# Routed attention and cosine-routed experts: turns of three units instead of two, and the PSUM banks shared out anew

## The chip, the cores and the metric

The kernel runs on one core of a Trainium2 chip. The metric is the device time of one execution in microseconds (us), 787.95 for the kernel before (median of three; 787.69 to 789.35). The engines are TensorE (PE in the profile, PEld for its weight loads), VectorE (DVE), ScalarE (ACT), GpSimd (POOL) and SyncE (SP, which here only issues DMA). Each has its own queue of instructions and they meet through semaphores. [...]

## What is computed

Attention over 4 images (batch) of 8 heads, 768 positions, 64 dimensions; a query sees only those keys that have the same nearest centroid of 16. Its result, as 3072 rows of 512, goes through a router with 8 experts, where one expert per row is taken.

```
q_assign = argmax(q_n . c_n);  k_assign = argmax(k_n . c_n)          # 16 centroids per head
scores   = where(q_assign == k_assign, q k^T / 8, -1e9)
attn_out = softmax(scores) v
x        = attn_out as rows (B*S, H*D) = (3072, 512)
e        = argmax(x_n . emb_n / tau);  gate = softmax(...)[e]
out      = gate * relu(x w1[e]) w2[e]                                # w1 512x1024, w2 1024x512
```

## The kernel before, in words

**Attention.** Two heads form a *pair*, 16 pairs in all (four per image), and each pair is worked in two halves of the queries. One half of one pair is a *group* of six *units*; a unit is 128 keys against 384 queries, of both heads. There are 192 units and 32 groups. For a unit, `scores` (L423) runs on PE: a bf16 product of one-hot numbers `kH` and `H`, which adds the mask, and an f32 product of `kT` and `qT`, into a two-bank PSUM tile `s_ps` (pool psS, two such tiles). `expo` (L445) takes the exponential on ACT into `prob` in SBUF (pool pp, five buffers). `attend` (L450) multiplies `v` with `prob` on PE and adds up over the six units in `o_ps` (pool psO, two banks), and lets DVE add the `prob` up in `acc`.

**A turn.** The main loop (L1003) goes over the units two at a time. In one turn it issues the scores and exponentials of the *next* two units, then what `between` (L935) and `early` (L914) hang into this turn, then `attend` for these two units. So PE has six turns per pair, 96 in all.

**A group's end.** `total` (L479) multiplies ones with `acc` to sum over partitions, into a bank of psM; DVE turns the sums (`sums`, L510) and inverts them (`inv`), POOL copies them to place (L514). `divide` (L519) turns them back (`den`) and forms `xT` from `o_ps`, the mean part `ev` and `den`. In the last three groups, `den` is copied by ACT and inverted whole by DVE (L503). `rows` (L540) turns `xT` and writes it to the DRAM tensor `x_rows`.

**Preparation of the next pair.** `prep_pieces` (L290): `turn0`, `turn1` turn q and k on DVE; `products` (L315) multiplies them with the centroids on PE into a bank of psM, which DVE empties with the transpose `asn` (L328); `choose` (L330) finds the cluster on DVE and writes its number into `cd` on ACT, and a transposing DMA makes `H` (`hot`) of it; `keys` (L372) copies `kH` out of it on POOL; `values` adds v up on POOL.

**Routing.** While image b is attended, image b-1 is routed by `route_pieces` (L554): products with the expert vectors (L559), logits, norms, choose, gates. `Places` (L652) works out where each row stands among its expert's rows; part a covers the first two images and is done in the third and fourth, part b the rest. All PE results of these go into one of the two banks of psM, handed out by `misc()` (L133).

**Experts.** After the last pair, blocks of 128 rows go through `hidden` (w1, L861) and `result` (w2, L880), with `turn_x` (L853) ahead; some 28 blocks are run. `result` sums in a bank of psO.

**What sets the order.** The stretch up to the first expert blocks is written out by hand for all engines (`manual_schedule`, L1001): every engine runs its instructions in the order of the code. The blocks from L1091 on are ordered by a scheduler. PSUM before: psO 2 banks, psM 2, psS 4. When attention is over, psS is given up and its four banks serve the expert part (psX 1, psH 3).

Of the kernel before, what the change touches and what calls it, by code (L numbers as in the profile page):

```python
# [18 lines left out]
P = 128  # L19
# [20 lines left out]
def kernel(  # L40
# [55 lines left out]
    io_i = const.tile([P, P], I32, name="io_i")  # L96
# [22 lines left out]
    xp = ctx.enter_context(tc.tile_pool(name="xp", bufs=2))  # L119
    rta = ctx.enter_context(tc.tile_pool(name="rta", bufs=1))  # L120
    xip = ctx.enter_context(tc.tile_pool(name="xip", bufs=3))
    psO = ctx.enter_context(tc.tile_pool(name="psO", bufs=2, space=PSUM))
    psM = ctx.enter_context(tc.tile_pool(name="psM", bufs=2, space=PSUM))
    at = ctx.enter_context(ExitStack())
    ldp = at.enter_context(tc.tile_pool(name="ldp", bufs=2, side="right"))
    trp = at.enter_context(tc.tile_pool(name="trp", bufs=2, side="right"))
    pp = at.enter_context(tc.tile_pool(name="pp", bufs=5, side="right"))
    ats = ctx.enter_context(ExitStack())
    psS = ats.enter_context(tc.tile_pool(name="psS", bufs=2, space=PSUM, side="right"))

    def misc():  # L133
        return psM.tile([P, 512], F32, tag="misc", name="misc")

    pairs = [(b, hp) for b in range(B) for hp in range(NHP)]
    ld = {}
# [53 lines left out]
    def constants():  # L191
        nc.vector.memset(onesb, 1.0)
        keep_up(9)
        nc.vector.memset(epsc, EPS)
        make_identity(nc, ident)
        nc.gpsimd.iota(io_i, pattern=[[1, P]], base=0, channel_multiplier=0)
# [24 lines left out]
        nc.vector.tensor_scalar(prefc, io_b[:, 0:C], -1.0, float(C), ALU.mult, ALU.add)  # L221
        nc.vector.tensor_scalar(prefe, io_b[:, 0:E], -1.0, float(E), ALU.mult, ALU.add)
# [34 lines left out]
    def begin():  # L257
# [11 lines left out]
        norm_rows(cn_r, c_sb, P)  # L269
        unit_centroids()  # L270
        keep_up(2)
        piece(0, "turn0")
        piece(0, "turn1")
        norm_rows(en_r, emb, E)

        nc.scalar.activation(cn_r, epsc, ACTF.Exp)
        piece(0, "products")
        for m in range(2):
            scores(m, (1,))
        piece(0, "choose")  # L280
        keep_up(6)
        piece(0, "turn_numbers")
        for m in range(2):
            scores(m, (0,))
            expo(m)
        piece(0, "values")
# [126 lines left out]
        }  # L413


    GU = NJ
    units = [(n, hq, j) for n in range(len(pairs)) for hq in range(2) for j in range(NJ)]
    ngroups = len(units) // GU
# [4 lines left out]
    def scores(i, parts=(0, 1)):  # L423
# [1 line left out]
        n, hq, j = units[i]  # L425
        t = ld[n]
        if "s_ps" not in un[i]:
            un[i]["s_ps"] = psS.tile([P, 2, 512], F32, tag="s_ps", name="s_ps")
        s_ps = un[i]["s_ps"]
        for part in parts:  # L430
            if part == 0:
# [18 lines left out]
    def attend(i):  # L450
# [13 lines left out]
        if j == 1:  # L464
            g["acc"] = xp.tile([P, 2, HS], F32, tag="acc", name="acc")
            nc.vector.scalar_tensor_tensor(  # L466
                out=g["acc"],
                in0=un[i - 1]["prob"],
                scalar=NJ * EPS,
                in1=d["prob"],  # L470
                op0=ALU.add,
                op1=ALU.add,
            )
            un[i - 1].clear()
        elif j > 1:
            nc.vector.tensor_tensor(g["acc"], g["acc"], d["prob"], ALU.add)  # L476
            d.clear()

    def total(g):  # L479

# [38 lines left out]
    def divide(g):  # L519
# [8 lines left out]
        if (b, hq) not in xT:  # L528
            xT[b, hq] = xp.tile([P, NHP, HS], F32, tag="xT", name="xT", bufs=3)
        nc.vector.scalar_tensor_tensor(  # L530
            out=xT[b, hq][:, hp],
            in0=d["o_ps"][:, 0:HS],
            scalar=ld[n]["ev"],
            in1=d["den"],
            op0=ALU.add,
# [344 lines left out]
    def result(j, halves=(0, 1)):  # L880
        d = mo[j]
        for half in halves:
            if half == 0:
                d["y_ps"] = psO.tile([P, DM], F32, tag="o_ps", name="y_ps")
            bk = d["y_ps"]
            for c in range(KF // 2 * half, KF // 2 * half + KF // 2):
                nc.tensor.matmul(  # L887
# [24 lines left out]
    prepare, route = {}, {}  # L912
    pa = Places(0, rta)
    early = {  # L914
        (2, 2, 1): pa.ranks,
        (2, 2, 3): pa.firsts,
        (2, 2, 5): pa.experts,
        (2, 3, 1): lambda: pa.dest(0),
        (2, 3, 3): lambda: pa.dest(1),
        (2, 3, 5): pa.hot_blocks,  # L920
        (3, 0, 1): lambda: pa.hot_rows(0, 4),
        (3, 0, 3): lambda: pa.hot_rows(1, 4),
        (3, 0, 5): lambda: pa.hot_rows(2, 4),
        (3, 1, 1): lambda: pa.hot_rows(3, 4),
        (3, 2, 2): pa.tokens,
        (3, 2, 3): lambda: (fetch(0), fetch(1), fetch(2)),
    }

    def piece(n, name, *args):
# [5 lines left out]
    def between(n, it):  # L935
        b, nb = divmod(n, NHP)
        if n == 0:

            if it == 0:
                piece(1, "turn0")  # L940
                piece(1, "turn1")
            elif it == 1:
                piece(1, "products")
                bk = misc()
                piece(0, "mean", bk)
                piece(0, "mean_out", bk)
            elif it == 2:
                piece(1, "choose")
                turned_experts()
        elif it == 0:  # L950
            piece(n + 1, "products")
        elif it == 1:
            piece(n + 1, "choose")
            rows(2 * n - 2)
        elif it == 3:
            rows(2 * n - 1)
        if it == 3:
            piece(n + 1, "keys")
        if it == 4:
            piece(n + 2, "turn0")  # L960
            piece(n + 1, "values")
        elif it == 5:
            piece(n + 2, "turn1")
        if b > 0:
            if nb == 0 and it == 3:
# [3 lines left out]
            m = NJ * nb + it  # L969
            if m in (5, 9, 12):  # L970
                read((m - 5) // 3 * 2, (m - 5) // 3 * 2 + 2)
            if m in (8, 9, 11, 12, 14, 15):
                norms((8, 9, 11, 12, 14, 15).index(m))
            if (nb, it) == (0, 3):
                products(0)
            elif (nb, it) == (0, 4):
                products(1)
            elif (nb, it) == (1, 2):
                logits(0)
            elif (nb, it) == (1, 3):  # L980
                logits(1)
            elif (nb, it) == (1, 4):
                choose()
            if 16 <= m < 20:
                gates[m - 16]()
        if n == NP - 1 and it == 4:
            route[b] = route_pieces(b)
            route[b][2](0, NJ, 0, DM - P)
        if b == B - 1 and (nb, it) == (3, 0):
            for j in range(2):  # L990
                weights1(j)
                weights2(j)
# [7 lines left out]
    }  # L1000
    with tc.manual_schedule(engines=by_hand):  # L1001
        begin()
        for i in range(0, len(units), 2):  # L1003
            n, it = divmod(i // 2, NJ)
# [4 lines left out]
            if it == 3 and n in (1, 2, 3, 5, 6, 7, 9, 10):  # L1009
# [14 lines left out]
            if (b, nb, it) in early:  # L1024
                early[b, nb, it]()
# [7 lines left out]
            if i + 2 == len(units):  # L1033
# [12 lines left out]
        total(ngroups - 1)  # L1046
        divide(ngroups - 1)
        rows(ngroups - 1)
# [114 lines left out]
```

The softmax here doesn't subtract the row's maximum and nothing guards it: scores larger than these inputs give would overflow.

## Time and profile before

The time before is 787.95 us; the profiled execution spans 786.4 us, at a granted clock of 0.997.

| stretch (us) | what runs | PE busy | DVE busy | ACT busy |
|---|---|---|---|---|
| 0 to 20 | constants, first pair's preparation | 14.75 of 20 | 10.52 | 10.11 |
| 100 to 120 | attention, image 1 | 20.00 of 20 | 16.89 | 9.95 |
| 240 to 260 | attention, image 2, places begin | 18.87 of 20 | 19.16 | 13.04 |
| 340 to 360 | end of attention | 19.02 of 20 | 15.30 | 11.56 |
| 460 to 480 | experts | 20.00 of 20 | 1.38 | 2.57 |

The profile tells the busy time of each engine; matmuls are pipelined and their ends are modelled, so what counts for PE is the distance from the start of one to the start of the next. A row like `o_ps<-prob,v 128x384 f32 x8` names the tile written, the tiles read, the shape, and how many instructions were merged. An f32 product appears as two matmuls (two passes). "Idle before <- releaser" tells what an engine waited for.

### The profile page before, as it was taken

To read this page: it belongs to the slowest core of one execution; us is meant where nothing else is said; L and a number is where in the kernel's file an instruction comes from. 1 tells how busy PE (TensorE), PEld (TensorE's weight loads), DVE (VectorE), ACT (ScalarE), POOL (GpSimd) and SP (SyncE) were. 2 spreads that over 40 slices of the span, in tenths; PEclk is the share of its full clock that TensorE was granted. 3 is DMA by queue.
4 is the path that set the end of the run, shared out by engine and by line. 5 is a ranking of instruction groups with operands and counts; after the bars stand their busy time and mean duration, and the time that the engine had idled before them with its cause. 6 is when DMAs were issued, how large, how long until landed. Compare 5 with 4: busy or idle time off the path is not lost.

```text
span 786.4 us, 12732 instructions
## 1 busy us (share of the span) xinstructions
PE 768.4 (98%) x4850; PEld 442.3 (56%) x4850; DVE 349.8 (44%) x614; ACT 259.7 (33%) x417; POOL 183.1 (23%) x402
## 2 busy tenths in 40 slices
PE   7999999999999999999999999999999999999995
PEld 3444444443444334436776776776776776776772
DVE  5688889998889998878430000000000000000000
ACT  5445455564457455563151111111110111111110
POOL 3233323434344233440111211211211211211200
PEclk9999999999999999999999999999999999999998
DMA  9466878877869456485797965988656763146400
GB/s 154 74 131 139 145 110 151 156 148 150 128 140 202 74 92 118 105 248 121 267 332 273 372 226 206 320 320 312 212 220 241 259 244 133 51 143 237 149 15 24
DMA packets 241888, 140.42 MB, mean 179 GB/s; under 512 B 202389, under 2 KB 203925, under 8 KB 241824
## 3 DMA queue, kind: packets, MB, share of 16 engines
q1 hardware_dynamic: 233968, 117.27, 58.5%
q0 software_dynamic: 4480, 13.87, 4.9%
q10 hardware_dynamic: 3376, 8.44, 3.1%
q8 instruction: 40, 0.66, 0.4%
q14 instruction: 24, 0.20, 0.1%
HBM read 158.61 MB, written 13.83 MB: 219 GB/s over the span
## 4 chain that ended last, share of the span: by engine, by line
PE 41%; issue 28%; DMA 23%; DVE 5%; POOL 1%; ACT 0%; SPq 0%; POOLq 0%; DVEq 0%; ACTq 0%
PE s_ps L437 17%; DMA out_dram<-y,sidx 17%; PE o_ps L457 14%; PE h_ps L871 3%; DMA out_dram<-y,gidx 2%; DVE acc L476 2%; PE y_ps L887 2%; PE misc L491 2%; PE misc L319 1%; DMA x_rows<-gate 1%; DMA w1s<-in_moe_w_dram 1%; PE misc L566 1%; DMA w2s<-in_moe_w_dram 1%; DMA q<-in_q_dram 1%; DMA k<-in_k_dram 1%
## 5 line engine op out<-in xcount | busy, mean ns | idle before, releaser
L871 PEld LDWEIGHTS h_ps<-xTm,w1s 128*128 128x128 f32 x1792 | 202.6, 192 | 20.8 <-DVE xTm L859 18.0
L871 PE MATMUL h_ps<-xTm,w1s 128*128 128x128 f32 x1792 | 208.0, 277 | 0.0
L887 PE MATMUL y_ps<-w2s,hT 128*128 128x512 f32 x448 | 201.1, 593 | 0.0
L448 ACT ACTIVATE prob<-s_ps 128x768 f32<-128x768 f32 x192 | 153.8, 810 | 143.1 <-PE s_ps L437 122.4
L859 DVE COPY xTm<-x_ps 128x512 f32<-128x512 f32 x24 | 16.6, 691 | 330.9 <-PE x_ps L857 330.9
L437 PE MATMUL s_ps<-qT,kT 64*128 64x384 f32 x768 | 155.1, 483 | 0.0
L457 PE MATMUL o_ps<-prob,v 128*64 128x384 f32 x768 | 145.1, 499 | 0.8 <-DVE xT L530 0.8
L476 DVE TENSOR_TENSOR acc<-acc,prob 128x768 f32<-128x768 f32 x128 | 129.6, 1012 | 6.4
L887 PEld LDWEIGHTS y_ps<-w2s,hT 128*128 128x128 f32 x448 | 81.0, 190 | 81.8 <-issue 81.8
L878 ACT ACTIVATE hT<-h_ps 128x512 f32<-128x512 f32 x56 | 33.4, 597 | 204.0 <-PE h_ps L871 204.0
L457 PEld LDWEIGHTS o_ps<-prob,v 128*64 128x64 f32 x768 | 46.5, 136 | 84.5 <-issue 69.4
L898 POOL DMA_INDIRECT out_dram<-y,sidx x24 | 23.8, 990 | 290.3 <-ACT y L897 284.4
L514 POOL COPY inv<-inv 32x6 f32<-32x6 f32 x232 | 56.2, 242 | 114.2 <-DVE inv L511 103.5
L437 PEld LDWEIGHTS s_ps<-qT,kT 64*128 64x128 f32 x768 | 68.8, 189 | 20.9 <-issue 20.6
L897 ACT ACTIVATE y<-y_ps,xin 128x512 f32<-128x512 f32 x28 | 19.2, 686 | 146.4 <-PE y_ps L887 140.1
L437 PE MATMUL s_ps<-hot,kH 64*128 64x384 bf16 x384 | 63.5, 328 | 2.3 <-ACT prob L448 1.3
L437 PEld LDWEIGHTS <-kH 64*128 64x128 bf16 x384 | 19.4, 93 | 64.0 <-issue 45.2
L375 POOL COPY kH<-hot 128x768 bf16<-128x768 bf16 x15 | 14.2, 947 | 95.5 <-DMA hot<-cd 83.0
L821 POOL DMA_INDIRECT xin<-x_rows,gidx x28 | 29.8, 1063 | 25.9 <-DMA x_rows<-gate 9.1
L466 DVE SCALAR_TENSOR_TENSOR acc<-prob 128x768 f32<-128x768 f32 x32 | 30.3, 947 | 0.0
L857 PEld LDWEIGHTS x_ps<-ident,xin 128*128 128x128 f32 x112 | 13.9, 141 | 13.8 <-issue 13.2
L491 PE MATMUL misc<-acc,ones 128*32 128x192 f32 (+1 forms) x244 | 18.0, 346 | 2.5 <-DVE acc L476 2.4
(192 smaller groups left out, 413.7 us busy)
## 6 DMA issues: line engine op xcount, KB each, us to landing
w1s<-in_moe_w_dram SPq DMA_DIRECT2D x28, 2048.0 KB
w2s<-in_moe_w_dram SPq DMA_DIRECT2D x28, 2048.0 KB
v<-in_v_dram SPq DMA_DIRECT2D x32, 192.0 KB
x_rows<-xb SPq DMA_DIRECT2D x128, 48.0 KB
q<-in_q_dram SPq DMA_DIRECT2D x60, 96.0 KB
k<-in_k_dram SPq DMA_DIRECT2D x60, 96.0 KB
xr<-x_rows SPq DMA_DIRECT2D x9, 512.0 KB
w1s<-in_moe_w_dram ACTq DMA_DIRECT2D x4, 1024.0 KB
```

Of the source, the lines that this page charges most:

```text
L437: nc.tensor.matmul(s_ps[:, h, 0:HS], lhsT=l[rows, P * j : P * j + P], rhs=r[rows], start=part == (1 if len(parts) < 2 else 0), stop=part = ...
L448: nc.scalar.activation(d["prob"], d["s_ps"][:, :, 0:HS], ACTF.Exp, scale=scale)
L457: nc.tensor.matmul(g["o_ps"][D * h : D * h + D, 0:HS], lhsT=ld[n]["v"][:, j, h], rhs=d["prob"][:, h], start=(j == 0), stop=(j == NJ - 1),)
L466: nc.vector.scalar_tensor_tensor(out=g["acc"], in0=un[i - 1]["prob"], scalar=NJ * EPS, in1=d["prob"], op0=ALU.add, op1=ALU.add,)
L476: nc.vector.tensor_tensor(g["acc"], g["acc"], d["prob"], ALU.add)
L491: nc.tensor.matmul(bk[M * i : M * i + M, 0:W], lhsT=ones[:, 0:M], rhs=d["acc"][:, i * W // HS, c : c + W], start=True, stop=True,)
L514: nc.gpsimd.tensor_copy(inv2[M * to : M * to + M, W // SQ * (i % 2) : W // SQ * (i % 2 + 1)], inv[M * i : M * i + M],)
L821: nc.gpsimd.indirect_dma_start(out=xin, out_offset=None, in_=x_rows[0:n], in_offset=bass.IndirectOffsetOnAxis(ap=gidxs[part][:, c : c + 1] ...
L871: nc.tensor.matmul(bk[:, m : m + P], lhsT=w1s[j % 2][:, c, f0 + m : f0 + m + P], rhs=d["xT"][:, P * c : P * c + P], start=(c == 0), stop=( ...
L878: nc.scalar.activation(d["hT"][:, f0 : f0 + 512], bk, ACTF.Relu)
L887: nc.tensor.matmul(bk, lhsT=d["hT"][:, P * c : P * c + P], rhs=w2s[j % 2][:, c], start=(c == 0), stop=(c == KF - 1),)
L898: nc.gpsimd.indirect_dma_start(out=out[:], out_offset=bass.IndirectOffsetOnAxis(ap=to, axis=0), in_=y, in_offset=None, bounds_check=N - 1, ...
```

## The change

Six units that were three turns become two. A turn has three units; a pair has four turns (NT) and PE 64 in all. For that, psS gets three two-bank tiles (6 banks), and psO and psM keep one bank each. So that the one `o_ps` bank is free for the next group, ACT copies the finished result to SBUF (`o_sb`), and `divide` reads it there. `prob` gets eight buffers. During the start, two of the scores' tiles serve as four spare banks for `misc()`. The pieces in `between` and `early` are hung anew on turns: products and choose of the next pair into turn 0, keys and values into turn 2, the transposes of the pair after into turn 3; the places go one to a turn from the twelfth turn of the third image. `total` and `divide` take turns. When attention is over, the expert part gets two banks of its own for results (psY) from the six of psS. The first product with the expert vectors for the last image moves from the last turn to behind the first half of the first hidden layer. The tile `io_i` moves into a pool that has room at the start.

```diff
-    psO = ctx.enter_context(tc.tile_pool(name="psO", bufs=2, space=PSUM))
-    psM = ctx.enter_context(tc.tile_pool(name="psM", bufs=2, space=PSUM))
+    psO = ctx.enter_context(tc.tile_pool(name="psO", bufs=1, space=PSUM))
+    psM = ctx.enter_context(tc.tile_pool(name="psM", bufs=1, space=PSUM))
...
-    pp = at.enter_context(tc.tile_pool(name="pp", bufs=5, side="right"))
+    pp = at.enter_context(tc.tile_pool(name="pp", bufs=8, side="right"))
...
-    psS = ats.enter_context(tc.tile_pool(name="psS", bufs=2, space=PSUM, side="right"))
+    psS = ats.enter_context(tc.tile_pool(name="psS", bufs=3, space=PSUM, side="right"))
+    spare = []
     def misc():
+        if spare:
+            return spare.pop(0)
         return psM.tile([P, 512], F32, tag="misc", name="misc")
...
+        for bk in (scores_bank(), scores_bank()):
+            spare.extend(bk[:, i] for i in range(2))
         piece(0, "turn0")
         piece(0, "turn1")
...
+    T, NT = 3, 2 * NJ // 3
...
+        if j == NJ - 1:
+            g["o_sb"] = xp.tile([P, HS], F32, tag="o_sb", name="o_sb")
+            nc.scalar.copy(g["o_sb"], g["o_ps"][:, 0:HS])
...
         nc.vector.scalar_tensor_tensor(
             out=xT[b, hq][:, hp],
-            in0=d["o_ps"][:, 0:HS],
+            in0=d["o_sb"],
...
-                d["y_ps"] = psO.tile([P, DM], F32, tag="o_ps", name="y_ps")
+                d["y_ps"] = psY.tile([P, DM], F32, tag="y_ps", name="y_ps")
...
-        (2, 2, 1): pa.ranks,
-        (2, 2, 3): pa.firsts,
-        (2, 2, 5): pa.experts,
-        (2, 3, 1): lambda: pa.dest(0),
-        (2, 3, 3): lambda: pa.dest(1),
-        (2, 3, 5): pa.hot_blocks,
-        (3, 0, 1): lambda: pa.hot_rows(0, 4),
...
+        (2, 11): pa.ranks,
+        (2, 13): pa.firsts,
+        (2, 14): pa.experts,
+        (2, 15): lambda: pa.dest(0),
+        (3, 1): lambda: pa.dest(1),
+        (3, 2): pa.hot_blocks,
+        (3, 3): lambda: pa.hot_rows(0, 4),
...
+        (3, 10): lambda: (fetch(0), fetch(1), fetch(2)),
...
         elif it == 0:
             piece(n + 1, "products")
+            piece(n + 1, "choose")
         elif it == 1:
-            piece(n + 1, "choose")
             rows(2 * n - 2)
+        elif it == 2:
+            rows(2 * n - 1)
+        if it == 2:
+            piece(n + 1, "keys")
+            piece(n + 1, "values")
         elif it == 3:
-            rows(2 * n - 1)
-        if it == 3:
-            piece(n + 1, "keys")
-        if it == 4:
             piece(n + 2, "turn0")
-            piece(n + 1, "values")
-        elif it == 5:
             piece(n + 2, "turn1")
...
-            if 16 <= m < 20:
-                gates[m - 16]()
+            if m in (1, 3):
+                products(m // 2)
+            elif m in (5, 7):
+                logits(m // 2 - 2)
+            elif m == 9:
+                choose()
+            elif m >= 12:
+                gates[m - 12]()
...
-            for m in range(i + 2, min(i + 4, len(units))):
+            for m in range(i + T, min(i + 2 * T, len(units))):
                 scores(m)
                 expo(m)
             between(n, it)
-            if i > GU and i % GU == (2 if i // GU + 2 >= ngroups else 4):
-                divide(i // GU - 1)
...
-            for m in range(i, i + 2):
+            for m in range(i, i + T):
                 attend(m)
-            if i + 2 == len(units):
+            if i > 0 and i % GU == 0:
+                total(i // GU - 1)
+            elif i > GU:
+                divide(i // GU - 1)
+            if last:
                 rows(ngroups - 2)
-                route[b][0](0)
-            if i % GU == 0 and i > 0:
-                total(i // GU - 1)
...
+        psY = ctx.enter_context(tc.tile_pool(name="psY", bufs=2, space=PSUM, **tile_waits))
...
         hidden(0, (0,))
+        products(0)
         total(ngroups - 1)
```

More of the change, by code (lines that the diff above doesn't have):

```diff
@@ L95 @@
     epsc = const.tile([P, 1], F32, name="epsc")
-    io_i = const.tile([P, P], I32, name="io_i")
     io_b = const.tile([P, P], BF16, name="io_b")
@@ L126, with scores_bank @@
     trp = at.enter_context(tc.tile_pool(name="trp", bufs=2, side="right"))
-    pp = at.enter_context(tc.tile_pool(name="pp", bufs=5, side="right"))
+    pp = at.enter_context(tc.tile_pool(name="pp", bufs=8, side="right"))
     ats = ctx.enter_context(ExitStack())
-    psS = ats.enter_context(tc.tile_pool(name="psS", bufs=2, space=PSUM, side="right"))
+    psS = ats.enter_context(tc.tile_pool(name="psS", bufs=3, space=PSUM, side="right"))
+    spare = []
     def misc():
+        if spare:
+            return spare.pop(0)
         return psM.tile([P, 512], F32, tag="misc", name="misc")
+    def scores_bank():
+        return psS.tile([P, 2, 512], F32, tag="s_ps", name="s_ps")
     pairs = [(b, hp) for b in range(B) for hp in range(NHP)]
@@ L195, in constants @@
         make_identity(nc, ident)
+        io_i = xp.tile([P, NJ, DM], F32, tag="xr", name="io", bufs=1).bitcast(I32)[:, 0, 0:P]
         nc.gpsimd.iota(io_i, pattern=[[1, P]], base=0, channel_multiplier=0)
@@ L277, in begin @@
         piece(0, "products")
-        for m in range(2):
+        for m in range(T):
             scores(m, (1,))
@@ L281, in begin @@
         keep_up(6)
+        spare.append(psO.tile([P, 512], F32, tag="o_ps", name="numbers_ps"))
         piece(0, "turn_numbers")
-        for m in range(2):
+        for m in range(T):
             scores(m, (0,))
@@ L427, in scores @@
         if "s_ps" not in un[i]:
-            un[i]["s_ps"] = psS.tile([P, 2, 512], F32, tag="s_ps", name="s_ps")
+            un[i]["s_ps"] = scores_bank()
         s_ps = un[i]["s_ps"]
@@ L914 @@
     early = {
-        (2, 2, 1): pa.ranks,
-        (2, 2, 3): pa.firsts,
-        (2, 2, 5): pa.experts,
-        (2, 3, 1): lambda: pa.dest(0),
-        (2, 3, 3): lambda: pa.dest(1),
-        (2, 3, 5): pa.hot_blocks,
-        (3, 0, 1): lambda: pa.hot_rows(0, 4),
[L922 to L926, printed above, removed]
+        (2, 11): pa.ranks,
[5 more added lines that the diff above has]
+        (3, 3): lambda: pa.hot_rows(0, 4),
+        (3, 5): lambda: pa.hot_rows(1, 4),
+        (3, 6): lambda: pa.hot_rows(2, 4),
+        (3, 7): lambda: pa.hot_rows(3, 4),
+        (3, 9): pa.tokens,
+        (3, 10): lambda: (fetch(0), fetch(1), fetch(2)),
     }
@@ L941, in between @@
                 piece(1, "turn1")
-            elif it == 1:
-                piece(1, "products")
                 bk = misc()
@@ L946, in between @@
                 piece(0, "mean_out", bk)
+            elif it == 1:
+                piece(1, "products")
+                piece(1, "choose")
             elif it == 2:
-                piece(1, "choose")
                 turned_experts()
@@ L951, in between @@
             piece(n + 1, "products")
+            piece(n + 1, "choose")
         elif it == 1:
-            piece(n + 1, "choose")
             rows(2 * n - 2)
+        elif it == 2:
[3 more added lines that the diff above has]
+            piece(n + 1, "values")
         elif it == 3:
-            rows(2 * n - 1)
-        if it == 3:
-            piece(n + 1, "keys")
-        if it == 4:
             piece(n + 2, "turn0")
-            piece(n + 1, "values")
-        elif it == 5:
             piece(n + 2, "turn1")
+        m = NT * nb + it
         if b > 0:
-            if nb == 0 and it == 3:
+            if m == 1:
                 route[b - 1] = route_pieces(b - 1)
             products, logits, read, norms, choose, gates = route.get(b - 1, (None,) * 6)
[L969 to L982, printed above, removed]
+            if m in (3, 6, 9):
+                j = (3, 6, 9).index(m) * 2
+                read(j, j + 2)
+            if m in (5, 6, 8, 9, 11, 12):
+                norms((5, 6, 8, 9, 11, 12).index(m))
+            if m in (1, 3):
[3 more added lines that the diff above has]
+            elif m == 9:
                 choose()
-            if 16 <= m < 20:
-                gates[m - 16]()
-        if n == NP - 1 and it == 4:
+            elif m >= 12:
+                gates[m - 12]()
+        if n == NP - 1 and it == 3:
             route[b] = route_pieces(b)
             route[b][2](0, NJ, 0, DM - P)
-        if b == B - 1 and (nb, it) == (3, 0):
+        if b == B - 1 and m == 12:
             for j in range(2):
@@ L1002 @@
         begin()
-        for i in range(0, len(units), 2):
-            n, it = divmod(i // 2, NJ)
+        for i in range(0, len(units), T):
+            n, it = divmod(i // T, NT)
             if it == 0 and n + 2 < NP:
@@ L1008 @@
                 load(n + 1, "v")
-            if it == 3 and n in (1, 2, 3, 5, 6, 7, 9, 10):
+            if it == 2 and n in (1, 2, 3, 5, 6, 7, 9, 10):
                 slot, part = divmod(n - 1 - n // 4, 4)
@@ L1020 @@
             between(n, it)
-            if i > GU and i % GU == (2 if i // GU + 2 >= ngroups else 4):
-                divide(i // GU - 1)
             b, nb = divmod(n, NHP)
-            if (b, nb, it) in early:
-                early[b, nb, it]()
-            if i + 2 == len(units):
+            if (b, NT * nb + it) in early:
+                early[b, NT * nb + it]()
+            last = i + T == len(units)
+            if last:
                 ats.close()
@@ L1030 @@
                 turn_x(0, nc.scalar.copy, xp.tile([P, DM], F32, tag="acc", name="xTm"))
-            for m in range(i, i + 2):
+            for m in range(i, i + T):
                 attend(m)
-            if i + 2 == len(units):
+            if i > 0 and i % GU == 0:
+                total(i // GU - 1)
+            elif i > GU:
+                divide(i // GU - 1)
+            if last:
                 rows(ngroups - 2)
-                route[b][0](0)
-            if i % GU == 0 and i > 0:
-                total(i // GU - 1)
         at.close()
```

## The prediction

> **What bounds the kernel now.** I read the busy shares first, then the 40 slices, then the matmuls in order of time inside the attention, then the waits, and last the stretch in which attention gives way to the experts.
>
> ```profile
> PE 768.4 (98%) x4850; PEld 442.3 (56%) x4850; DVE 349.8 (44%) x614; ACT 259.7 (33%) x417; POOL 183.1 (23%) x402
> ...
> PE   7999999999999999999999999999999999999995
> ...
> DVE  5688889998889998878430000000000000000000
> ```
>
> TensorE is busy from end to end, so only three things can shorten the kernel: fewer or cheaper matmuls, less lost between matmuls, or the few stalls. VectorE (DVE) is next in the attention (slices 1 to 18), near full in slices 12 to 14, and nearly idle afterwards. This is one turn of the attention as TensorE runs it, two units:
>
> ```profile
> 150.75 0.33 PE L437 MATMUL s_ps<-hot,kH 64*128 64x384 bf16 x2
> 150.91 0.81 PE L437 MATMUL s_ps<-qT,kT 64*128 64x384 f32 x4
> 151.65 1.51 PE L457 MATMUL o_ps<-prob,v 128*64 128x384 f32 x8
> 153.09 0.34 PE L437 MATMUL s_ps<-hot,kH 64*128 64x384 bf16 x2
> 153.27 0.81 PE L437 MATMUL s_ps<-qT,kT 64*128 64x384 f32 x4
> ```
>
> The first column is the start. A plain turn is 3.16 us (151.65 to 154.81 for the next L457). The starts of single matmuls say where it goes: inside a block the next pass starts 0.161 us later for the bf16 mask part and 0.322 us for each f32 pass, so the scores of a unit take 0.161 + 2 x 0.322 = 0.806 us and its attend 2 x 0.322 = 0.645 us. Two units make 2.90; the turn takes 0.26 more. That is lost at the two changes of kind: 0.415 instead of 0.322 from the last score pass to the first attend pass, 0.374 at the next attend pass, 0.425 from the last attend pass back to the scores, and 0.174 for 0.161 at the first mask part: 0.093 + 0.052 + 0.103 + 0.012 = 0.26 us.
>
> Where TensorE really stops is found by the same starts: nine of them between 24 and 352 us come later than the same change does elsewhere, at 180.0 (0.64), 253.1 (0.42), 258.1 (0.85), 266.4 (0.35), 267.5 (0.31), 269.3 (0.71), 336.0 (0.13), 344.6 (0.63) and 347.3 (0.51): 4.5 us. Six of the nine lie at or after the first placing steps. The waits of 240 to 285 us name DVE, which has 19.1 of 20 us busy there:
>
> ```profile
> 240.00:260.00 20.00, 18.87 (x134) 7.86 (x132) 19.16 (x40) 13.04 (x21) 6.13 (x15) 1.00 1.05 192
> 260.00:280.00 20.00, 18.95 (x128) 7.49 (x126) 19.12 (x43) 9.62 (x14) 7.82 (x21) 1.00 0.59 90
> ```
>
> The columns are PE, weight loads, DVE, ACT, POOL. PE is short of 20 just where DVE is full. At the change to the experts nothing stalls today:
>
> ```profile
> 362.67 1.51 PE L457 MATMUL o_ps<-prob,v 128*64 128x384 f32 x8
> 364.11 0.85 PE L566 MATMUL misc<-xT,embT 128*32 128x384 f32 x8
> 364.89 3.84 PE L871 MATMUL h_ps<-xTm,w1s 128*128 128x128 f32 x32
> 368.66 0.87 PE L491 MATMUL misc<-acc,ones 128*64 128x384 f32 x4
> ```
>
> [...]
>
> **The change part by part.**
>
> *Turns of three.* 192 units make 64 turns instead of 96. The matmuls are the same; 32 pairs of changes go: 32 x 0.26 = **-8.3 us**, all on the path. In a pair of heads this is 20.99 to 20.47 us. The extra pieces (products, sums) keep their own changes.
>
> *One result bank, with a copy.* Each of 32 groups gains a 128x384 ScalarE copy, 0.48 us by the row of the den copy from PSUM, 15 us in all on an engine a half busy. The copy follows the group's last attend; the next attend comes after three scores, 2.4 us. Cost nothing: the scores hide it. DVE's divide no longer holds the bank, which removes the 0.63 us stall at 344.6.
>
> *Lighter turns, eight probability buffers, later transposes.* An exponential may now run when DVE is one turn of 4.6 us behind, formerly one of 3.2; sums wait for additions a turn earlier, likewise. The nine stalls should go: **-4.5 us**.
>
> *One bank for others.* Now every user of it waits until the one before has been emptied. I step DVE through a pair of four turns with the starts of its rows: asn .5, choose 2.0, acc .95 per unit, sums .6, rows .5, divide 1.1, the two transposes 1.85. With no routing it ends turns 0 to 3 at 8.3, 12.8, 16.3 and 23.0 us from the pair's start, against TensorE's 6.2, 10.8, 15.9 and 20.5; the next products come at 20.5 + 3.2, so asn is not late and the sums (at 5.4 in turn 0) find the bank empty. In the fourth pair of the third image turn 1 gets the gate scale (1.1) and the first blocks (1.6), turn 3 the gate sum (1.0) and the places (.7): DVE ends it near 27.4, so 6.9 us into the next pair, and empties products at 7.5. The sums behind it wait 2.2 us; the routed products of turn 1 then wait some 1.1 for the sums. The durations overlap by up to a tenth each, so I take 2.5 of the 3.3: **+2.5 us** (bounds 0 and 5).
>
> *Root at the start of a pair.* On ScalarE the two table loads and the root (2.8 us) now stand behind the mask numbers of choose; that puts turn 1's exponentials at about 10.2 us and turn 2's scores want them at 11.0. I take .3 for each of two images: **+0.6** (0 to 2).
>
> *The first pair.* Its keys were wanted six turns after the start with choose in turn 2; now choose is in turn 1 and the keys are wanted in turn 3. From the transposing DMA to the key copy took 4.0 us (28.1 to 32.1), the copy .8. With choose done near 28 the keys stand at 33.1, and TensorE is there at 31.8: **+1.2** (0 to 2).
>
> *The start.* Four spare banks for the first transposes remove the wait at 7.81 us (0.32) and its emptying: **-0.5**.
>
> *The last pair and the hand-over.* The last three divisors use a full reciprocal of 2.55 us on DVE. Its last turns hold three of these and 11.6 us of additions behind in-order waits: the reciprocal of the third-last group starts at 6.2 us into the pair (after the root and the den copy), the additions of turn 1 end at 13.0, the second reciprocal runs 16.1 to 18.7, gate sum and additions end at 22.5, and the divide at 23.0. TensorE has finished its attends and half a hidden layer at 21.5 and wants this for products(0): 1.5. Then the sums of the last group wait for the copy of that bank, 0.3 + 0.48: 0.8. Then products(1) waits for the reduce of logits(0) in the same bank: 0.4. **+2.7 us** (1 to 5).
>
> *Banks for experts.* Two before, two after, in other places; the order of matmuls after the hand-over is the same. Nothing, since y is emptied 7 us before its bank is wanted. The tiles that only moved (io) cost nothing, at the start behind the loads.
>
> Sum: 787.95 - 8.3 - 4.5 - 0.5 + 2.5 + 0.6 + 1.2 + 2.7 = **781.7 us**.
>
> **The rivals.** *All new waits outside the hand-over hide:* 787.95 - 13.3 + 2.7 = 777.4. For it: the longer turns forgive more. Against: DVE has only 1.4 us of slack in a pair. *DVE takes over in the third and fourth image:* only the first two gain from turns (4.2 us) and the stalls stay: 787.95 - 4.2 - 0.5 + 1.2 + 2.7 = 787.2. For it: 19.1 of 20 us. Against: work moves out of that stretch into the fourth image. *Slower:* the single bank is late in each of the 11 other pairs of the routed images, at half of my 2.5 us: 781.7 + 13.8 = 795.5. For it: sums stand right behind products. Against: by my steps asn is there 0.9 us early or more in ordinary pairs.
>
> **How the numbers follow.** Forecast 0.6, all hidden 0.2, DVE-bound 0.12, slower 0.08. The range, 777.0 to 787.5, takes in the first three and the bounds of the unknown waits; about two in ten lie outside, since the bounds can add up. Bounds of no change are 786.4 and 789.5: faster 0.82, same 0.09 (most of the DVE case), slower 0.09.
>
> **What would show it.** Right: a plain turn of 4.61 us; a pair of heads of 20.5; no late starts of the old nine; a wait of the mean or sums for asn in the pair after the places; a late start of the routing products behind the first hidden half. Wrong: late starts at every pair's sums, exponentials held behind the mask numbers, or the attend of a new group waiting for the copy of the old one; and a plain turn over 4.7 us would sink the first term.

## The result and the profile after

The changed kernel takes 793.96 us (793.78 to 794.22) beside 788.19 us of the kernel before on the same chip: a ratio of 1.0071 (95% interval 1.0054 to 1.0089). It is slower by 0.7%; the forecast was 781.7 us. The span of the profiled execution grows from 786.4 to 792.4 us, so the two traces have 6.0 us to explain.

The page of the changed kernel, busy shares and two rows of the 40 slices:

```profile
PE 763.9 (96%) x4850; PEld 449.6 (57%) x4850; DVE 353.9 (45%) x614; ACT 271.5 (34%) x449; POOL 201.5 (25%) x402
...
PE   7999999999999989969999999999999999999995
...
PEclk9999999999999999998999999999999999999998
```

TensorE is busy for 4.5 us less than before, although the span is longer: what was to be saved between matmuls has been saved, and more has been lost in stops. The eighteenth slice (337 to 357 us) has a 6 where the kernel before had a 9, and the granted clock (PEclk) falls in the nineteenth. The same in numbers, per 20 us: PE, weight loads, DVE, ACT, POOL, then the clock, the DMA share and GB/s.

```profile
340.00:360.00 20.00, 13.07 (x78) 6.04 (x76) 8.96 (x14) 9.92 (x15) 4.03 (x10) 0.82 0.72 257
360.00:380.00 20.00, 18.75 (x127) 11.71 (x127) 15.59 (x19) 5.93 (x11) 0.00 (x0) 0.93 0.37 86
```

The matmuls of TensorE, in order of time, show one stop that is larger than the whole loss:

```profile
347.95 2.16 PE L470 MATMUL o_ps<-prob,v 128*64 128x384 f32 x12
357.03 0.51 PE L450 MATMUL s_ps<-hot,kH 64*128 64x384 bf16 x2 [6.93 <-ACT prob L461]
357.31 1.51 PE L450 MATMUL s_ps<-qT,kT 64*128 64x384 f32 x4
```

After an attend the scores normally start 2.1 us later; here it is 9.1, so 7.0 us are lost. (Below, the time given for a stop is the start of the last matmul before it, and its size is how much later than elsewhere the next one starts.) Then four f32 score passes take 1.51 us instead of 0.81: single passes start 0.640 us apart instead of 0.322. That is half the clock (granted clock 0.50), it lasts until 362.9 us, and it costs a further 2.9 us.

The stop can be followed back. TensorE waits for ScalarE's exponentials, which empty the banks of the scores. Here are ScalarE's and then VectorE's instructions of the same stretch:

```profile
345.08 0.21 ACT L637 ACTIVATE sq<-sq 128x6 f32<-128x6 f32 x1
354.38 0.48 ACT L518 COPY den<-misc 128x384 f32<-128x384 f32 x1 [9.09 <-DVE ev L412]
354.88 1.28 ACT L461 ACT_TABLE_LOAD   x1
356.17 2.21 ACT L461 ACTIVATE prob<-s_ps 128x768 f32<-128x768 f32 x3
```

```profile
351.11 0.58 DVE L540 STREAM_TRANSPOSE den<-inv 128x384 f32<-128x384 f32 x1 [10.26 <-POOL inv L530]
351.73 0.62 DVE L546 SCALAR_TENSOR_TENSOR xT<-o_sb,ev,den 128x384 f32<-128x384 f32 x1
352.26 0.95 DVE L479 SCALAR_TENSOR_TENSOR acc<-prob 128x768 f32<-128x768 f32 x1
353.32 0.96 DVE L489 TENSOR_TENSOR acc<-acc,prob 128x768 f32<-128x768 f32 x1
354.19 0.15 DVE L412 COPY ev<-misc 128x1 f32<-128x1 f32 x1
```

ScalarE's exponentials stand behind a table load of 1.28 us and, before that, its copy of the divisor, which waits for VectorE's ev copy, which stands behind a transposition (den) that has waited 10.3 us for the copies of the reciprocals on GpSimd. And these are GpSimd's instructions, after and then before:

```profile
329.64 3.75 POOL L634 TENSOR_TENSOR cumx<-cumx,eq 128x8 bf16<-128x8 bf16 x6
333.33 0.82 POOL L386 COPY kH<-hot 128x768 bf16<-128x768 bf16 x1
334.12 1.31 POOL L395 TENSOR_TENSOR vs<-v 128x384 f32<-128x384 f32 x1
...
337.87 1.99 POOL L837 DMA_INDIRECT xin<-x_rows,gidx  x1 [0.17 <-DVE sums L526]
340.17 1.57 POOL L837 DMA_INDIRECT xin<-x_rows,gidx  x1 [0.31 <-issue]
342.04 1.00 POOL L837 DMA_INDIRECT xin<-x_rows,gidx  x1 [0.30 <-issue]
343.04 0.41 POOL L530 COPY inv<-inv 32x6 f32<-32x6 f32 x2
349.78 1.30 POOL L530 COPY inv<-inv 32x6 f32<-32x6 f32 x6 [6.32 <-DMA xin<-x_rows,gidx]
```

```profile
335.83 1.77 POOL L821 DMA_INDIRECT xin<-x_rows,gidx  x1 [0.17 <-issue]
337.91 1.00 POOL L821 DMA_INDIRECT xin<-x_rows,gidx  x1 [0.31 <-issue]
339.21 0.99 POOL L821 DMA_INDIRECT xin<-x_rows,gidx  x1 [0.30 <-issue]
340.21 0.42 POOL L514 COPY inv<-inv 32x6 f32<-32x6 f32 x2
343.06 1.30 POOL L514 COPY inv<-inv 32x6 f32<-32x6 f32 x6 [2.43 <-DMA xin<-x_rows,gidx]
```

In both kernels the third copy of the reciprocals waits until the tokens that the three fetches bring have landed. Nothing in the source makes the copies need the tokens. The first two copies run right behind the fetches; it is the third that carries, in both traces, waits for the three semaphores that the fetches raise. Why the build puts them there stays open. Before, the wait was 2.43 us. In the changed kernel the fetches are issued 2.0 to 2.8 us later, since the running counts (L634, 3.75 us) and the values' sums (L395 to L397) now stand right ahead of them on GpSimd. They landed at 340.5, 342.2 and 342.9 us before, and land at 342.2, 348.2 and 349.6 now. In between four expert weights of 2 MB each are on the move, issued by SyncE from 338.88 us, before the second fetch; before, the first of them was issued at 340.67, after the third.

### The profile page after: what moved, and what is told of

Same layout as the page of the kernel before. It is cut to its first block, busy times and chain, and to the rows that moved or that the text cites. A ratio compares the mean times of both kernels' runs of the same rounds, so it can differ in the third digit from the quotient of the medians.

```text
span 792.4 us, 12802 instructions
## 1 busy us (share of the span) xinstructions
PE 763.9 (96%) x4850; PEld 449.6 (57%) x4850; DVE 353.9 (45%) x614; ACT 271.5 (34%) x449; POOL 201.5 (25%) x402
## 4 chain that ended last, share of the span: by engine, by line
issue 33%; PE 27%; DMA 21%; DVE 12%; SPq 2%; POOL 2%; ACT 1%; POOLq 0%; DVEq 0%; ACTq 0%
DMA out_dram<-y,sidx 16%; PE s_ps L450 11%; PE o_ps L470 8%; DVE acc L489 4%; PE h_ps L887 2%; DMA out_dram<-y,gidx 2%; PE y_ps L903 2%; DVE acc L479 1%; DMA x_rows<-gate 1%; SPq L162 1%; PE misc L507 1%; DMA k<-in_k_dram 1%; DMA xin<-x_rows,gidx 1%; PE misc L330 1%; DVE xT L546 1%
## 5 line engine op out<-in xcount | busy, mean ns | idle before, releaser
L461 ACT ACTIVATE prob<-s_ps 128x768 f32<-128x768 f32 x192 | 151.0, 813 | 57.1 <-PE s_ps L450 53.1
L450 PE MATMUL s_ps<-qT,kT 64*128 64x384 f32 x768 | 157.0, 488 | 0.0
L470 PE MATMUL o_ps<-prob,v 128*64 128x384 f32 x768 | 138.4, 496 | 0.5 <-ACT o_sb L493 0.5
L489 DVE TENSOR_TENSOR acc<-acc,prob 128x768 f32<-128x768 f32 x128 | 127.2, 994 | 9.5 <-ACT junk L617 0.5
L530 POOL COPY inv<-inv 32x6 f32<-32x6 f32 x232 | 62.3, 269 | 165.1 <-DVE inv L527 150.5
L470 PEld LDWEIGHTS o_ps<-prob,v 128*64 128x64 f32 x768 | 49.6, 137 | 79.0 <-issue 67.4
L479 DVE SCALAR_TENSOR_TENSOR acc<-prob 128x768 f32<-128x768 f32 x32 | 34.3, 1073 | 0.0
L493 ACT COPY o_sb<-o_ps 128x384 f32<-128x384 f32 x32 | 15.4, 480 | 32.9 <-PE o_ps L470 32.8
L395 POOL TENSOR_TENSOR vs<-v 128x384 f32<-128x384 f32 x16 | 21.0, 1315 | 9.7 <-DMA v<-in_v_dram 8.9
L540 DVE STREAM_TRANSPOSE den<-inv 128x384 f32<-128x384 f32 x29 | 16.6, 572 | 13.0 <-POOL inv L530 13.0
```

What stands on the lines that cost most here:

```text
L395: nc.gpsimd.tensor_tensor(vs, v[:, 0 : NJ // 2], v[:, NJ // 2 :], ALU.add)
L450: nc.tensor.matmul(s_ps[:, h, 0:HS], lhsT=l[rows, P * j : P * j + P], rhs=r[rows], start=part == (1 if len(parts) < 2 else 0), stop=part = ...
L461: nc.scalar.activation(d["prob"], d["s_ps"][:, :, 0:HS], ACTF.Exp, scale=scale)
L470: nc.tensor.matmul(g["o_ps"][D * h : D * h + D, 0:HS], lhsT=ld[n]["v"][:, j, h], rhs=d["prob"][:, h], start=(j == 0), stop=(j == NJ - 1),)
L479: nc.vector.scalar_tensor_tensor(out=g["acc"], in0=un[i - 1]["prob"], scalar=NJ * EPS, in1=d["prob"], op0=ALU.add, op1=ALU.add,)
L530: nc.gpsimd.tensor_copy(inv2[M * to : M * to + M, W // SQ * (i % 2) : W // SQ * (i % 2 + 1)], inv[M * i : M * i + M],)
```

## The experiments

Below, "the changed kernel" is at a ratio of 1.0071, and every ratio is to the kernel before in the same batch of runs. Its median lay between 788.19 and 789.74 us from batch to batch, so ratios are the better measure across batches.

### The fetches behind the copies (e1) and the weights a turn later (e2)

```diff
-        (3, 10): lambda: (fetch(0), fetch(1), fetch(2)),
+        (3, 11): lambda: (fetch(0), fetch(1), fetch(2)),
```

> The changed kernel with one edit: the three fetches stand one turn later, at turn 11 of the last image instead of turn 10, so that in GpSimd's queue they come after the copies of the inverted sums of that turn and no such copies follow them. Queue theory (the copies wait for the landing of the fetches, and all else queues behind): the stop of 7.0 us at 349.6 and the half clock after it (some 2.9 us) go, 793.96 becomes about 784.1. Rival (VectorE is full and one bank for others is too few; the fetch only shows it): at most 2 us, about 792. Rival (the root and its table loads in front of the last pair's exponentials): the stop stays at 4 us or more, about 790.

Measured 784.84 us, ratio 0.9943 (0.9929 to 0.9958). Three instructions, one turn later, take 1.28% off, about 10 us (9.1 between the two medians, which come from different batches); the stop and the half clock after it were 7.0 + 2.9 = 9.9. GpSimd in e1:

```profile
338.53 3.65 POOL L530 COPY inv<-inv 32x6 f32<-32x6 f32 x8 [0.27 <-DVE inv L527]
342.48 1.25 POOL L837 DMA_INDIRECT xin<-x_rows,gidx  x1 [0.29 <-POOL inv L530]
...
345.50 1.00 POOL L837 DMA_INDIRECT xin<-x_rows,gidx  x1 [0.30 <-issue]
```

The eight copies run ahead of the fetches, nothing in this stretch waits for a landing, and TensorE has no stop between 329 and 362 us. This shows the cause of the loss: the fetches' place ahead of the copies. e2 leaves the fetches where the change put them and moves the weights:

```diff
-        if b == B - 1 and m == 12:
+        if b == B - 1 and m == 13:
```

> The changed kernel with one edit: the first blocks' weights are asked for one turn later (turn 13 instead of 12 of the last image); the fetches stay. Queue theory: the 8 MB of weights no longer stand in front of the second and third fetch, which land in some 3 us instead of 7.6 after the last was issued; the copies go on 4 us sooner, the stop falls from 7.0 to about 3 us, 793.96 becomes about 789.5 (a little less if the clock then stays whole). Rival (VectorE full, one bank): no change, 794. If the fetches land as late as before, the length of the wait is not the weights'.

Measured 792.65 us, ratio 1.0041 (1.0023 to 1.0060): 1.3 us better, less than expected. GpSimd, then TensorE, then a later line of VectorE and TensorE's wait for it:

```profile
345.99 1.30 POOL L530 COPY inv<-inv 32x6 f32<-32x6 f32 x6 [2.30 <-DMA xin<-x_rows,gidx]
```

```profile
353.24 0.37 PE L450 MATMUL s_ps<-hot,kH 64*128 64x384 bf16 x2 [2.88 <-ACT prob L461]
353.40 1.49 PE L450 MATMUL s_ps<-qT,kT 64*128 64x384 f32 x4
...
377.17 1.42 PE L582 MATMUL misc<-xT,embT 128*32 128x384 f32 x8 [2.57 <-DVE lg L598]
378.52 4.88 PE L887 MATMUL h_ps<-xTm,w1s 128*128 128x128 f32 x32
```

```profile
376.39 0.58 DVE L561 STREAM_TRANSPOSE xb<-xT 128x384 f32<-128x384 f32 x1 [2.56 <-DMA x_rows<-xb]
```

The landing wait falls from 6.3 to 2.3 us, and TensorE's stop from 6.9 to 2.9: so 4 of the 7 us came with the weights in flight, and the rest is the place in GpSimd's queue. But 2.9 us of stop are still followed by the half clock (1.49 us for four passes): the three units' scores take 4.2 us and not 2.5, so 1.7 of the 2.9 us stay. And the weights, now issued from 357.8 us, stand just ahead of the writing of the last rows, which SyncE issues from 361.1: VectorE waits 2.6 us for one of these writes to land, TensorE's second routing products 2.6 instead of 0.3, and half clock follows here too (1.42 us for 0.85, and 4.88 for the 3.84 of the next hidden half). So 4.1 and 1.2 us were gained, 2.2 and 1.6 given back later: 1.5, and 1.3 were measured.

### The same hazard in the kernel before (e5)

```diff
-        (3, 2, 3): lambda: (fetch(0), fetch(1), fetch(2)),
+        (3, 2, 4): lambda: (fetch(0), fetch(1), fetch(2)),
```

> This is the kernel before, with one edit: the first three fetches of tokens are issued one turn (two units) later in the last image, behind the copies of the reciprocals and not ahead of them. Theory (the copies on GpSimd carry a wait for the landing of the fetches, and the two late starts of TensorE near 344.6 and 347.3 us of the kernel before, 1.1 us together, are its end): these two late starts go, the 2.4 us wait of GpSimd and the 2.5 us wait of VectorE go with it, and the time falls by about 1.1 us, a ratio of 0.9986. Rival, which is what the prediction took (these late starts come from the result bank that is freed late, as at the other seven places): both stay, ratio 1.000.

Measured 788.40 us over 21 runs against 789.58, ratio 0.9988 (0.9981 to 0.9995). The late starts near 344.6 and 347.3 us are gone from its trace. (That trace has a stop of its own, 2.6 us near 253 us for GpSimd's copy of the keys, and half clock from 15.6 to 22.4 us, both far from the edit; it is of the longest of the 21 executions.) So the hazard was there already, worth 0.12%, and two of the nine stalls that the prediction booked were its end. The wait that named it (GpSimd for the fetches, 2.43 us) stands in the trace of before, and the prediction doesn't use it.

### The root (e3, e9)

e3 is e1 without the root of the first three images' norms; a copy stands in its place:

```diff
-            nc.scalar.activation(t["sq"], t["sq"], ACTF.Sqrt)
+            nc.scalar.activation(t["sq"], t["sq"], ACTF.Copy if b < B - 1 else ACTF.Sqrt)
```

> The kernel with the later fetch, and the square root of the first three images' norms left out (a copy stands in its place, so no tables are loaded in the attention). If the two table loads behind the mask numbers hold the next exponentials, the late starts of scores at 174.9 (0.6) and 260.1 (1.5) go and the kernel gains about 2.1 us on the kernel with the later fetch. Rival (these scores wait for VectorE's additions to free the probability buffers): no gain, within 0.3 us.

Measured 784.00 us, ratio 0.9930 (0.9912 to 0.9949), 0.8 us less than e1. In e1 the scores start 0.7 and 1.5 us late at 175 and 260 us, behind exponentials that stand behind two table loads; both late starts are gone in e3. But the mean's wait in the last pair of the third image grew from 2.0 to 2.7 us, and 0.4 us appeared at 264. The stops were the root's, and more than half of what it frees is lost again: a few turns later to VectorE, and in this trace to a longer half clock (277.9 to 284.7 us, in e1 280.6 to 284.0). e9 moves the four steps of the gates one turn, away from the turn in which ScalarE waits for the choice of hot keys (it is built on e8, below):

```diff
-            elif m >= 12:
-                gates[m - 12]()
+            elif m >= 13:
+                for gate in gates[m - 13 : m - 12 if m < 15 else None]:
+                    gate()
```

> e8, and the four steps of the gates one turn later (turns 13 to 15 and not 12 to 15, the last two in one turn), so that the root with its two table loads no longer lies in the turn in which ScalarE waits 2 us for VectorE's choice of hot keys. Theory (the root costs TensorE 0.7 and 1.5 us at 174 and 260 us because it adds 2.7 us to a turn in which ScalarE has already lost 2): these stops go, and with the same in the fourth image up to 2.2 us less than e8; since e3 gave back most of what the root's removal freed, at the bank of the last pair, and that bank is now free earlier, 1.3 to 2.2 us less. Rival 1 (two table loads of 1.28 us delay three exponentials wherever they lie): stops of the same size at turn 13, no change. Rival 2 (VectorE, not ScalarE, sets the pace there): the stop returns elsewhere, under 0.8 us less.

Measured 783.56 us, ratio 0.9928 (0.9913 to 0.9944), 0.3 us less than e8, within the intervals. The stops at 174 and 260 us are gone, and 1.1 us each appear at 193 and 279, named for VectorE's sums: the second rival.

### The first pair (e4)

e4 is e1 with the next pair's products and choice put into the first turn of the first pair, and the mean of v one turn later:

```diff
             if it == 0:
                 piece(1, "turn0")
                 piece(1, "turn1")
+                piece(1, "products")
+                piece(1, "choose")
+            elif it == 1:
                 bk = misc()
...
-            elif it == 1:
-                piece(1, "products")
-                piece(1, "choose")
```

> The kernel with the later fetch, and in the very first pair the products and the choice for the second pair one turn sooner (turn 0), the mean part of v one turn later (turn 1). If the second pair's keys are late by the time from the choice through the transposing DMA, the late start at 32.4 (1.1 to 1.25 us) goes and the kernel gains about 1.2 us on the kernel with the later fetch. Rival (the products then wait for the transposes of q and k on VectorE, and the loss only moves): within 0.4 us of it.

Measured 783.64 us, ratio 0.9927 (0.9912 to 0.9941), 1.2 us less than e1. The late start at 32.7 us is gone, as its size said.

### The one bank and VectorE (e6, e8, e10, e11)

In e4 the largest stop that is left in the attention is this, TensorE in order of time:

```profile
274.63 2.16 PE L470 MATMUL o_ps<-prob,v 128*64 128x384 f32 x12
278.71 0.35 PE L402 MATMUL misc<-epsc,vs 128*128 128x1 f32 x2 [1.93 <-DVE asn L339]
...
279.71 1.49 PE L450 MATMUL s_ps<-qT,kT 64*128 64x384 f32 x4
```

The mean waits for the bank, since VectorE empties the products (asn, 277.99) 3.3 us after they were done; then the half clock again. e6 is e4 with the places moved:

```diff
-        (2, 13): pa.firsts,
-        (2, 14): pa.experts,
-        (2, 15): lambda: pa.dest(0),
-        (3, 1): lambda: pa.dest(1),
-        (3, 2): pa.hot_blocks,
+        (3, 0): lambda: (pa.firsts(), pa.experts()),
+        (3, 1): lambda: pa.dest(0),
+        (3, 2): lambda: (pa.dest(1), pa.hot_blocks()),
```

> The changed kernel with the fetches a turn later and the first pair's keys early (e4), and beside these the firsts, experts and destinations of the first two images' places moved out of the last pair of the third image into the first three turns of the fourth: some 4 us of VectorE work leave a stretch in which it is busy without a gap. Theory (the mean waits 2.0 us in the single bank at 277 us because VectorE is late, and the half clock of some 1.6 to 2.9 us behind it follows from that stop): both go, 3.6 to 4.5 us less than e4's 783.6, so 779.1 to 780.0. Rival 1 (the single bank alone makes the mean wait, however early VectorE is): the stop stays, no change, 783.6. Rival 2 (VectorE's work only moves and makes TensorE wait in the fourth image's first turns): one stop is traded for another, 782 to 784.

Measured 782.67 us, ratio 0.9918 (0.9904 to 0.9932), the lowest of all, though its interval overlaps that of e4. The mean comes on time (276.12) and the half clock is gone, but the next user of the bank waits:

```profile
276.12 0.38 PE L402 MATMUL misc<-epsc,vs 128*128 128x1 f32 x2
276.43 0.53 PE L507 MATMUL misc<-acc,ones 128*32 128x192 f32 x8
...
281.17 0.85 PE L582 MATMUL misc<-xT,embT 128*32 128x384 f32 x8 [1.67 <-DVE sums L526]
```

This is rival 2 of its expectation: one stop traded for another. e8 spreads the same steps over turns 1 to 3 of the fourth image:

```diff
-        (3, 0): lambda: (pa.firsts(), pa.experts()),
-        (3, 1): lambda: pa.dest(0),
-        (3, 2): lambda: (pa.dest(1), pa.hot_blocks()),
-        (3, 3): lambda: pa.hot_rows(0, 4),
+        (3, 1): lambda: (pa.firsts(), pa.dest(0)),
+        (3, 2): lambda: (pa.dest(1), pa.experts()),
+        (3, 3): lambda: (pa.hot_blocks(), pa.hot_rows(0, 4)),
```

> e6, with the moved places spread over turns of the fourth image that have no choosing of hot keys: firsts and the first destinations at turn 1, the second destinations and the experts at turn 2, the hot blocks with the first hot rows at turn 3. In e6 the mean's wait of 2.0 us in the one bank had gone, but the route's products, next in the same bank, waited 1.7 us for VectorE, which had 4 us of places between choosing and additions. Theory (whichever use of the one bank meets VectorE late waits, so the work must lie where nothing in the bank is near): the 1.7 us stop shrinks to under 0.5, and the 0.5 us at 291 with it, so 780.5 to 781.3 against e6's 782.7. Rival (VectorE is full over the whole stretch from 252 to 300 us, and the stop only moves on to the next turns): 782 to 783.5.

Measured 783.90 us, ratio 0.9933 (0.9918 to 0.9948): no gain. The stop of 1.7 us is gone, and one of 2.0 stands further on, before the routing's second products, at 289.9 us. The time lies a little above what even the rival gave. e10 (on e9) and e11 (on e8) put the places at the end of their turns, so that the bank's readers stand ahead of them in VectorE's queue:

```diff
-            if (b, NT * nb + it) in early:
-                early[b, NT * nb + it]()
             last = i + T == len(units)
...
             elif i > GU:
                 divide(i // GU - 1)
+            if (b, NT * nb + it) in early:
+                early[b, NT * nb + it]()
```

> e9 (root moved, places spread), and beside it each step of the places goes at the end of its turn, behind the turn's sums or division, and not ahead of its additions. VectorE takes its work in order, so in e9 the sums of the total at 287 us left the one bank only at 292, behind the places and the additions, and the route's products waited 2.1 us. Theory (the one bank costs time where its reader stands behind unrelated work in VectorE's queue; with the reader in front, the same amount of work costs nothing): the 2.1 us and 0.5 us stops at 291 and 304 go, about 2.4 us less than e9's 783.6, so 781.2. Rival (VectorE is full there and TensorE waits for it at another point): 782.5 to 783.6.

> e8 with the same edit of e10 and the root left where it was: the same theory expects about 2.4 us less than e8's 783.9, so 781.5, and the root's late starts at 174 and 260 us (0.9 and 0.8 us in e8) still there; the rival 783 to 784.

Measured 784.12 us (ratio 0.9940, 0.9927 to 0.9954) and 783.82 us (0.9930, 0.9917 to 0.9943). The 2.0 us at 290 us became 0.3 in e11, as the theory has it, but the list of waits of e11 shows where they went:

```profile
PE s_ps L450 <- ACT prob L461: 3.1, 3, 1.9
PE misc L402 <- DVE asn L339: 1.6, 1, 1.6
PE misc L330 <- DVE rka L700: 1.4, 1, 1.4
...
PE misc L595 <- DVE sums L526: 1.1, 1, 1.1
```

The columns are the sum, the count and the longest. The products at 251.7 now wait for the ranks in the bank, and the mean for asn two pairs later. Both times show no gain: the rival's outcome, in e10 0.5 us above its range. The reason that it gives is a full VectorE. Here is the busy time of e9, in which the scores hardly wait for exponentials (0.6 us in all), and below it a stretch of the changed kernel:

```profile
240.00:260.00 20.00, 19.90 (x144) 8.81 (x145) 19.00 (x32) 11.63 (x21) 9.26 (x22) 1.00 0.79 165
260.00:280.00 20.00, 19.25 (x140) 8.31 (x136) 18.93 (x31) 12.94 (x21) 7.44 (x18) 1.00 0.55 91
280.00:300.00 20.00, 17.20 (x126) 7.08 (x128) 18.76 (x48) 10.54 (x16) 7.60 (x21) 1.00 0.81 127
```

```profile
300.00:320.00 20.00, 19.98 (x144) 8.96 (x142) 19.17 (x32) 11.20 (x20) 9.33 (x20) 1.00 0.63 104
```

In e9 VectorE is busy for 56.7 us of 60, and TensorE stops. But from 300 to 320 us of the changed kernel it is busy for 19.17 us of 20, and TensorE hardly stops (19.98). So a full VectorE alone is not enough: it takes a use of the bank whose reader comes late in VectorE's order of work. That both are needed is argued from these traces and not tested by itself. In each of the five arrangements of the same work some use of the bank met a late reader; they lie between 782.7 and 784.1 us, and the lowest and the highest have overlapping intervals. What these runs leave open is how much two banks for others would have saved there: with six banks for scores there is no second one, and it wasn't tried.

### The hand-over (e7)

e7 is e6 with the last total moved:

```diff
         hidden(0, (0,))
         products(0)
+        hidden(0, (1,))
         total(ngroups - 1)
         divide(ngroups - 1)
         rows(ngroups - 1)
-        hidden(0, (1,))
```

> e6, and beside it the last group's total moved behind the second half of the first expert block's hidden layer, so that the one bank for others is free of the route's products when the total comes. Theory (the hand-over's 0.57 us before the total and the 0.25 to 0.35 us before the second products are waits in the one bank, which other work can fill): 0.6 to 0.9 us less than e6. Rival (the last image's route comes 3.7 us later for it and its places wait): the same as e6, or 1 to 3 us more.

Measured 788.63 us, ratio 0.9989 (0.9979 to 1.0000): 6 us slower than e6, so the rival, and more than it said. The 0.57 us before the total is hidden, as meant, but TensorE then waits 3.4 us for the first logits' reduce and, later, 1.4 us for tokens; there is half clock after the first (0.91 over 360 to 380 us). In VectorE's order of work the reduce (370.65 us) stands behind the last divisor's full reciprocal (366.91 us, 2.55 us long), which waits for this total.

## Why the prediction was wrong

- **The failed step.** The prediction's sum has no term for GpSimd and the fetches. It gave the stall at 344.6 us to a result bank held by the divide ("One result bank, with a copy") and under "Lighter turns" let all nine stalls go; the places, the fetches among them, were costed on VectorE alone. The runs put 7.0 us of stop and 2.9 us of half clock there (e1). Without these 9.9 us the changed kernel stands near 784 (e1: 784.84), inside the range given. That every engine runs its instructions in the order of the code does not give the first link, for two copies run right behind the fetches: that the third waits for their landing had to be taken from the trace of before (2.43 us). Given that wait, the order gives the rest, and the trace of the changed kernel shows it: the late copies hold VectorE (10.26 us), VectorE holds ScalarE (9.09), ScalarE holds TensorE (6.93).
- **Why the landing took so long.** It went with the weights in flight: with them the last fetch landed 7.6 us after its issue (342.04 to 349.6), with them a turn later (e2) at 345.85, 3.6 us after (342.27). In e1, with the weights ahead of them, all three took 7.0 to 7.1. How the transfers hold each other up was not measured.
- **Turns of three, -8.3.** Right: a plain turn is 4.61 us and a pair 20.48, against 20.99.
- **Nine stalls, -4.5.** Seven went; which part of the change took them away was not tested. The two at 344.6 and 347.3 us, 1.1 in all, had the other cause (e5), and it is that cause which returns as the 7.0. Eight of the nine, not six, lie after the first placing step (the ranks, 240.7 us).
- **The start, -0.5.** Wrong: the first mask parts wait for VectorE as long as before (1.01 us, before 1.00), and the wait that should go (0.32 us at 7.81) is 0.57 long; 0 in the sum below.
- **One bank for others, +2.5.** The place is right, and so is the order of events: the mean 2.0 us late at 276.7 and the routed products 1.2 at 282.0, which is nearly the 3.3 from before the discount for overlapping durations; a further 0.5 come later (293.6 and 305.6), 3.7 in all.
- **One result bank, 0.** Nearly right: once in 32 groups, at 166.8 us, the attend waited 0.5 us for the copy, which stood on ScalarE behind the norms of rows that had not been read yet.
- **Root, +0.6.** Mechanism right, size 2.1 (0.6 and 1.5): the two table loads (1.28 us each) fall in a turn in which ScalarE has already waited 2 us for the choice (e3, e9).
- **First pair, +1.2.** Right, 1.25 (e4).
- **Hand-over, +2.7.** Measured 1.4 (0.49, 0.57, 0.35); the full reciprocals delay the divide less than worked out.

The measured terms: -8.3 - 4.5 + 3.7 + 0.5 + 2.1 + 1.25 + 1.4 + 7.0 + 2.9 = +6.05, against 6.0 in the spans. The rival "slower" gave 795.5, close to the time by luck: its reason (the one bank late in eleven pairs) is not what happened, for ordinary pairs have no late sums.

## What to carry over

When a schedule is packed anew, list for each in-order queue what each waiting instruction stands in front of, GpSimd and the transfers included, and not only the two busiest engines. A wait of 2.4 us that costs 1.1 today (e5) has no fixed price: here the third copy came 6.7 us later (349.78 and not 343.06), and TensorE's stop grew by 5.9. Where VectorE was 94% full over 60 us, moving work about within that stretch moved the stop and did not remove it; the move that paid (e1, 10 us) took an instruction out of a chain.

## What was not expected of the hardware

After some of its stops TensorE ran at half its clock for several microseconds (single f32 passes 0.640 us apart instead of 0.322), which makes such a stop dearer than it looks: 7.0 us of stop cost 2.9 more, 2.9 us in e2 another 1.7, and 1.9 us of idling in e1 and e4 some 1.6. Half clock lasted 3.4 us in e1 (280.6 to 284.0), 6.8 us in e3 (277.9 to 284.7) and 10.2 us in the changed kernel (352.7 to 362.9, with TensorE stopped until 357.0).

The length of the stop alone does not decide it. The stop of the mean is as long in e1 as in the changed kernel (1.94 and 1.93 us of idling), and only e1 has half clock behind it. Here are stretches of 3.4 us around it, e1 first; the clock is the figure behind the five busy times:

```profile
277.14:280.55 3.41, 1.48 (x16) 0.82 (x16) 3.27 (x7) 0.00 (x0) 0.00 (x0) 1.00 1.13 159
280.55:283.97 3.42, 3.42 (x16) 1.61 (x12) 3.25 (x8) 2.33 (x5) 0.00 (x0) 0.50 0.23 36
```

```profile
274.14:277.55 3.41, 3.06 (x22) 0.93 (x20) 3.31 (x6) 1.05 (x2) 0.00 (x0) 1.00 0.73 110
277.55:280.97 3.42, 1.84 (x20) 1.19 (x22) 3.25 (x7) 0.00 (x0) 0.00 (x0) 1.00 1.08 135
280.97:284.38 3.41, 2.31 (x22) 0.74 (x18) 3.25 (x8) 3.04 (x6) 0.58 (x3) 1.00 0.35 68
```

In e1 the first stretch has 1.93 us of idling (3.41 less 1.48), and the second is at half clock, 0.50. In the changed kernel the clock stays at 1.00 in all three, though they hold the same stop and a second one of 1.10 us behind it. The stops of 2.0 us in e8 and 2.1 in e9 had no half clock behind them either (1.00 from 280 to 300 us in both), while those of 2.6 and 2.9 us in e2 and of 3.4 in e7 had. So in these traces a stop near 2 us cost some 1.6 us more, or nothing more. What decides between the two was not shown.
